# Two clamps to GpSimd, four weight splits to VectorE, and a later decode of the first weight blocks

## The chip, the cores and the metric

One core of a Trainium2 chip runs the whole program: one launch, inputs and output in the chip's memory. The metric is the device time of the program in microseconds. The median of three runs before the change is 835.16 us (833.45 to 838.1).

## What is computed

Three stages. The first is a linear attention with a decay per key channel, over 4 batches, 8 heads, 768 steps and 48 channels:

```python
for t in range(S):
    cur = np.einsum('bhd,bhe->bhde', u[None] * kt, vt)
    y[:, :, t] = np.einsum('bhd,bhde->bhe', rt, state + cur)
    state = wt[:, :, :, None] * state + np.einsum('bhd,bhe->bhde', kt, vt)
```

Its output, 3072 tokens by 384, goes through `h = x @ w_in`, `g = h * clip(h + 3, 0, 6) / 6`, `g @ w_out` with 2048 hidden columns, and then through a second feed-forward layer with 1024 hidden columns, a softmax-weighted `h`, a normalisation over the row with a gain, and a last product. The inputs of the attention are single precision. The weights are double precision in memory.

## The kernel before

**Attention.** The 768 steps are cut into 6 chunks of 128; a chunk of one batch is a tile, so there are 24 tiles, numbered chunk by chunk (tile `i` is batch `i % 4`). Each goes through six stages: `stw` (L410) clamps the decay to 0.75 to 1.25 and checks it on ScalarE; `st0` (L427) transposes decay and `r` on TensorE and forms running products with scans on VectorE; `st1` (L454) does the same for `k`, and forms `z = r * k * u` on GpSimd; `st2` (L495) makes the scores on TensorE and masks them into `am`; `st3` (L549) multiplies by `v`; `st4` (L603) writes the tile into the first feed-forward layer's input as a high and a low part. In the first four tiles one half of the masked scores is copied by ScalarE and then cut by GpSimd's affine select (L528). The clamped decay `wc` has one buffer, so a tile's clamp waits until the tile before has been transposed.

**Weights.** Each double is read as two 32-bit words. A block is 128 hidden columns of `w_in` and the matching rows of `w_out`, 768 values per partition, loaded by two transfers (`load_dec`, L25). `dec_a` (L35) clamps the high word, masks its sign (both on VectorE), and scales the clamped word on ScalarE. `dec_b` (L47) merges it with the sign and with the low word's top bits, two VectorE instructions (L50 and L53) that each read two tiles. `split` (L59) writes the high part on ScalarE and, as the difference, the low part on the engine that it is given (L61): GpSimd for every block. `w1_a` and `w1_b` (L354, L357) do this for the 16 blocks of the first layer; `w2_a` and `w2_b` for the 16 half-size blocks of the second, 384 values each. Raw words and decoded words have two buffers each.

**First feed-forward layer.** Six groups of 512 tokens times 16 blocks make 96 slots. In a slot `n`, `ffn_in` (L629) does nine products into `h`, ScalarE and VectorE make `t`, `gh` and `gl` of it (L643 to L647; `gl` on GpSimd in every other of the first 16 slots), and `ffn_out` (L650) does nine products two slots later. One attention tile goes through its stages for every four slots, so tile 4 and later ones run between the products. Slot `n` also decodes: `w1_b(n + LD)`, `w1_a(n + LD + 1)` and the load of block `n + LD + 2`, with `LD` 5 (L787 to L792). The second layer's weights are decoded in slots 78 to 94.

**Order.** The first four tiles and the first decodes run ahead of the slots in ten ticks (L753): in each tick every tile of the first four does its next stage (the tiles start at ticks 0, 2, 3 and 4), then the blocks of that tick's row of `decodes` follow, each with the rest of the block before it and the next load. In this part the queues of SP (which issues the loads) and of GpSimd keep the written order among themselves; on the other engines, and after `order.close()` on all, a scheduler chooses the order of the instructions from modelled costs. Each engine carries out its queue in order.

```python
decodes = {4: [0, 1], 5: [2], 6: [3], 7: [4], 8: [5]}
...
for m in decodes.get(tick, []):
    if m:
        w1_b(m - 1)
        w1_load(m + 1)
    w1_a(m)
```

The inputs of a tile have two buffers (tile 2's lie elsewhere), `v` from tile 4 on has four. `load_to` (L732) loads a later tile after `st1` in the ticks, and after `st2` in the slots.

Of the kernel before, what the change touches and what calls it, by code (L numbers as in the profile page):

```python
# [8 lines left out]
F32 = mybir.dt.float32  # L9
# [4 lines left out]
ALU = mybir.AluOpType  # L14
# [4 lines left out]
P = 128  # L19
W_LO, W_HI = 0.75, 1.25  # L20
SIGN = -(2**31)
HW_MAX = struct.unpack("<f", struct.pack("<I", 0x47EFF000))[0]
# [13 lines left out]
def dec_a(nc, pool, raw):  # L36

    f = pool.tile([P, raw.shape[1]], I32, tag="dec", name="dec", bufs=2)
    hw = raw[:, :, 1]
    nc.vector.tensor_scalar(  # L40
        out=f.bitcast(F32), in0=hw.bitcast(F32), scalar1=-HW_MAX, scalar2=HW_MAX, op0=ALU.max, op1=ALU.min
    )
    nc.vector.tensor_scalar(out=hw, in0=hw, scalar1=SIGN, scalar2=None, op0=ALU.bitwise_and)  # L43
    nc.scalar.activation(out=f.bitcast(F32), in_=f.bitcast(F32), func=ACTF.Copy, scale=2.0**-112)
    return f


def dec_b(nc, raw, f):

    nc.vector.scalar_tensor_tensor(  # L50
        out=f, in0=f, scalar=3, in1=raw[:, :, 1], op0=ALU.logical_shift_left, op1=ALU.bitwise_or
    )
    nc.vector.scalar_tensor_tensor(  # L53
        out=f, in0=raw[:, :, 0], scalar=29, in1=f, op0=ALU.logical_shift_right, op1=ALU.bitwise_or
    )
    return f.bitcast(F32)


def split(nc, src, hi, lo, eng):  # L59
    nc.scalar.activation(out=hi, in_=src, func=ACTF.Copy)  # L60
    eng.tensor_tensor(out=lo, in0=src, in1=hi.bitcast(F32), op=ALU.subtract)  # L61
# [206 lines left out]
def fast_path(  # L268
# [14 lines left out]
    nc = tc.nc  # L283
    B, H, S, D = r.shape
# [45 lines left out]
        out=causal.bitcast(F32), in_=ones, pattern=[[1, P]], compare_op=ALU.is_gt, fill=0.0, base=0,  # L330
# [3 lines left out]
    inp = right.enter_context(tc.tile_pool(name="inp", bufs=2, side="right"))  # L334
# [7 lines left out]
    w1_t = {}  # L342
    wst = {}
# [12 lines left out]

    def w1_b(m):  # L357
        w1_t[m] = w1p.tile([P, 2, WN], F32R, tag=f"w1_{m}", name="w1")
        split(nc, dec_b(nc, *wst.pop(m)), w1_t[m][:, 0, :], w1_t[m][:, 1, :], nc.gpsimd)


    s_st = []
# [30 lines left out]
    def load_v(i):  # L393
        g, b = divmod(i, B)
        if i < B:
            t = early(i, 1, H, D)
        else:
            t = inp.tile([P, H, D], F32, tag="v", name="v", bufs=4)
        nc.sync.dma_start(out=t, in_=v[b, :, g * C:(g + 1) * C, :].rearrange("h t d -> t h d"))
        at[i]["v"] = t  # L400

# [8 lines left out]
    def stw(i):  # L410
        a = at[i]
        wc = atp.tile([P, H, 64], F32, tag="wc", name="wc", bufs=1)
        flat = slice(0, H * 64 - 16)
        nc.vector.tensor_scalar(
            out=wc.rearrange("p h d -> p (h d)")[:, flat], in0=a["w"].rearrange("p h d -> p (h d)")[:, flat],
            scalar1=W_LO, scalar2=W_HI, op0=ALU.max, op1=ALU.min,
        )
        a["wc"] = wc
        junk = atp.tile([P, H, D], BF16, tag="junk", name="junk", bufs=1)
        nc.scalar.activation(  # L420
            out=junk, in_=a["w"][:, :, 0:D], func=ACTF.Relu, scale=-1.0, bias=b_lo, accum_out=chk[:, 3 * i:3 * i + 1]
        )
        nc.scalar.activation(
            out=junk, in_=a["w"][:, :, 0:D], func=ACTF.Relu, bias=b_hi, accum_out=chk[:, 3 * i + 1:3 * i + 2]
        )
# [309 lines left out]
            load_v(nxt[0])  # L735
            nxt[0] += 1

    LD = 5
    order = ctx.enter_context(ExitStack())
    order.enter_context(tc.manual_schedule(engines={mybir.EngineType.SP, mybir.EngineType.Pool}))  # L740
    load_in(0)
# [7 lines left out]
    w1_load(1)  # L749
    nxt[0] = 3  # L750
    starts = [0, 2, 3, 4]
    decodes = {4: [0, 1], 5: [2], 6: [3], 7: [4], 8: [5]}
    for tick in range(starts[-1] + 6):  # L753
        for i in range(B):
            s = tick - starts[i]
# [164 lines left out]
```

## Time and profile before

| | |
|---|---|
| median of three runs | 835.16 us |
| the profiled execution, its own time | 835.26 us |
| its span, from the first instruction to the last | 833.2 us |
| TensorE busy (share of the span) | 789.2 us (95%) |
| VectorE busy | 533.0 us (64%) |
| ScalarE busy | 350.0 us (42%) |
| GpSimd busy | 288.2 us (35%) |
| mean granted clock of TensorE | 0.958 of full speed |

In the profile PE is TensorE's products and PEld its weight loads, DVE is VectorE, ACT ScalarE, POOL GpSimd, SP the engine that issues loads and stores. Busy time is the time that an engine's instructions cover; an instruction that is held up inside its execution counts as busy. A line such as L50 is a line of the kernel, and `out<-in` are the program's names of tiles. In a row by line, the figures after the bar are the busy time of the group in us, the mean of one instruction in ns, and the idle time of the engine just before them with what ended it.

### The profile page before, as it was taken

The page shows a single profiled execution, that of the slowest core. Times are in us where ns is not written, and L with a number is a line of the kernel's source. Part 1 is how long each engine was busy: PE and PEld are TensorE (multiplying, and loading weights), DVE is VectorE, ACT ScalarE, POOL GpSimd, SP SyncE. Part 2 cuts the span into 40 slices and gives each one's busy share as a digit, 9 for nine tenths or more (in the row PEclk, how much of TensorE's full clock was granted, in tenths as well). Part 3 has the DMA queues.
Part 4 walks back from the last instruction along what each step waited for, and adds up shares of the span by engine and source line. Part 5 has one row for each costly group of instructions (what it writes and reads, how often), then busy time and mean ns, then how long its engine had stood idle before and what let it go on. Part 6 is the DMA issues. An engine that isn't in the chain of part 4 may idle for free.

```text
span 833.2 us, 12281 instructions
## 1 busy us (share of the span) xinstructions
PE 789.2 (95%) x4558; PEld 670.5 (80%) x4558; DVE 533.0 (64%) x988; ACT 350.0 (42%) x659; POOL 288.2 (35%) x379
## 2 busy tenths in 40 slices
PE   5779789999999999999999999998999999999996
PEld 5667577788888888888888888786789999999996
DVE  4989999756565555655556665699465555555552
ACT  2335644444334443343334333554443443344342
POOL 4385776634333332332233321122132222222210
PEclk7559997999999999999999999999999999999999
DMA  9765554214222322232222200433011111111101
GB/s 181 132 161 128 165 141 137 47 41 131 58 57 58 95 58 57 55 85 52 52 52 72 48 18 20 142 111 98 13 63 39 41 47 48 39 42 45 38 20 34
DMA packets 146117, 60.86 MB, mean 73 GB/s; under 512 B 103680, under 2 KB 140672, under 8 KB 146048
## 3 DMA queue, kind: packets, MB, share of 16 engines
q1 hardware_dynamic: 143456, 55.27, 27.1%
q10 hardware_dynamic: 2592, 4.72, 1.6%
q8 instruction: 38, 0.62, 0.3%
q14 instruction: 31, 0.25, 0.1%
HBM read 46.60 MB, written 13.37 MB: 72 GB/s over the span
## 4 chain that ended last, share of the span: by engine, by line
PE 73%; DVE 13%; issue 5%; ACT 3%; POOL 2%; DMA 2%; SPq 1%; POOLq 0%; ACTq 0%; DVEq 0%
PE y L659 19%; PE h L639 17%; PE po L856 12%; PE h L829 12%; DVE dec L50 3%; PE pt L843 2%; PE pa L519 2%; PE yt L570 2%; PE yt L576 2%; DVE dec L53 2%; PE kv L480 2%; DVE t L644 1%; DVE dec L40 1%; DVE raw L43 1%; DMA raw<-in_moe_w_in_dram 1%
## 5 line engine op out<-in xcount | busy, mean ns | idle before, releaser
L659 PE MATMUL y<-gh,w 128*128 128x512 f32 x576 | 204.4, 409 | 0.0
L639 PE MATMUL h<-xh,w 128*128 128x512 f32 x576 | 196.0, 394 | 4.6 <-DVE t L644 4.6
L639 PEld LDWEIGHTS h<-xh,w 128*128 128x128 f32 x576 | 109.0, 189 | 30.1 <-DVE t L644 7.1
L659 PEld LDWEIGHTS y<-gh,w 128*128 128x128 f32 x576 | 109.3, 190 | 27.8 <-issue 3.7
L643 ACT ACTIVATE t<-h,three 128x512 f32<-128x512 f32 x96 | 65.7, 685 | 151.2 <-PE h L639 151.2
L659 PE MATMUL y<-gl,w 128*128 128x512 f32 x288 | 114.3, 397 | 0.0
L639 PE MATMUL h<-xl,w 128*128 128x512 f32 x288 | 112.8, 392 | 0.0
L644 DVE SCALAR_TENSOR_TENSOR t<-t,h 128x512 f32<-128x512 f32 x96 | 65.3, 681 | 45.3 <-ACT t L643 45.3
L645 ACT ACTIVATE gh<-t 128x512 fp32r<-128x512 f32 x96 | 60.4, 629 | 73.9 <-DVE t L644 73.7
L647 DVE TENSOR_TENSOR gl<-t,gh 128x512 fp32r<-128x512 f32 x88 | 71.0, 807 | 29.6 <-ACT gh L645 28.0
L537 POOL TENSOR_TENSOR am<-ident,d 128x512 f32<-128x512 f32 x40 | 46.7, 1186 | 108.3 <-PE yt L576 107.4
L441 DVE TENSOR_TENSOR_SCAN q<-wt,ones 112x128 f32<-112x128 f32 x80 | 29.5, 409 | 69.3 <-PE wt L408 69.2
L67 DVE TENSOR_REDUCE nm<-h 128x1 f32<-128x1024 f32 x24 | 29.4, 1225 | 62.6 <-PE h L829 62.5
L856 PE MATMUL po<-w_oh,qh 128*128 128x384 f32 x192 | 67.0, 349 | 0.3 <-ACT qh L845 0.3
L856 PE MATMUL po<-w_oh,ql 128*128 128x384 f32 x192 | 65.2, 339 | 0.1
L856 PE MATMUL po<-w_ol,qh 128*128 128x384 f32 x192 | 65.0, 339 | 0.0
L639 PEld LDWEIGHTS h<-xl,w 128*128 128x128 f32 x288 | 54.5, 189 | 11.3
L659 PEld LDWEIGHTS y<-gl,w 128*128 128x128 f32 x288 | 55.0, 191 | 9.5 <-DVE gl L647 0.3
L845 ACT ACTIVATE qh<-pt 128x512 fp32r<-128x512 f32 x48 | 26.1, 595 | 79.0 <-PE pt L843 79.0
L829 PE MATMUL h<-w_ih,yl 128*128 128x512 f32 x144 | 56.6, 393 | 0.0
L829 PE MATMUL h<-w_il,yh 128*128 128x512 f32 x144 | 56.4, 392 | 0.0
L86 POOL TENSOR_TENSOR st<-st,mhalf 128x1 f32<-128x1 f32 x24 | 13.2, 552 | 124.0 <-DVE st L83 124.0
(123 smaller groups left out, 1483.8 us busy)
## 6 DMA issues: line engine op xcount, KB each, us to landing
raw<-in_moe_w_in_dram SPq DMA_DIRECT2D x24, 384.0 KB, 3.4
raw<-in_moe_w_out_dram SPq DMA_DIRECT2D x24, 384.0 KB, 4.1
w<-in_w_dram SPq DMA_DIRECT2D x24, 192.0 KB, 3.0
r<-in_r_dram SPq DMA_DIRECT2D x24, 192.0 KB, 3.2
k<-in_k_dram SPq DMA_DIRECT2D x24, 192.0 KB, 3.1
y1d<-ye ACTq DMA_DIRECT2D x18, 256.0 KB, 2.3
y<-y1d SPq DMA_DIRECT2D x24, 192.0 KB, 2.8
out_dram<-os SPq DMA_DIRECT2D x24, 192.0 KB, 1.9
```

The costliest lines, as they stand in the source:

```text
L67: nc.vector.tensor_reduce(out=nm, in_=h, axis=AX.X, op=ALU.max, negate=True)
L441: nc.vector.tensor_tensor_scan(out=q[0:DP, hp, 0:C][:, ::-1], data0=wt[0:DP, hp, :][:, ::-1], data1=ones[0:DP, :], initial=1.0, op0=ALU.mu ...
L537: nc.gpsimd.tensor_tensor(out=am, in0=ident.unsqueeze(1).to_broadcast([P, HP, C]), in1=dv[:, hh, :].unsqueeze(2).to_broadcast([P, HP, C]), ...
L639: nc.tensor.matmul(out=h, lhsT=a, rhs=b, start=(j == 0), stop=(j == len(ops) - 1))
L643: nc.scalar.activation(out=t, in_=h, func=ACTF.Relu, bias=three)
L644: nc.vector.scalar_tensor_tensor(out=t, in0=t, scalar=6.0, in1=h, op0=ALU.min, op1=ALU.mult)
L645: nc.scalar.activation(out=gh, in_=t, func=ACTF.Copy)
L647: eng.tensor_tensor(out=gl, in0=t, in1=gh.bitcast(F32), op=ALU.subtract)
L659: nc.tensor.matmul(out=y_ps[g][c], lhsT=a, rhs=b, start=(m == 0 and j == 0), stop=(m == M1 - 1 and j == 2))
L829: nc.tensor.matmul(out=h[:, fs], lhsT=a[:, c, :], rhs=b_[:, c, fs], start=(j == 0), stop=(j == len(ops) - 1))
L845: nc.scalar.activation(out=qh[:, ms, :], in_=pt, func=ACTF.Copy)
L856: nc.tensor.matmul(out=po, lhsT=x[:, m, :], rhs=y[:, m, :], start=(n == 0), stop=(n == 3 * M2 - 1))
```

## The change

Five edits. The clamp of the high words (`dec_a`, used by both layers' blocks) is issued by GpSimd, with its two bounds in the other order. The low part of the first four blocks (`m < B`, and `B` is 4) is formed on VectorE. The decay clamp is on GpSimd from tile 2 on. `v` has three buffers. Blocks are decoded four slots ahead, not five, and the ticks 4, 5, 7, 8 and 9 hold one block each, so that the loads of blocks 2 to 5 come in ticks 5, 7, 8 and 9.

```diff
--- before.py
+++ after.py
@@ -37,8 +37,8 @@
 
     f = pool.tile([P, raw.shape[1]], I32, tag="dec", name="dec", bufs=2)
     hw = raw[:, :, 1]
-    nc.vector.tensor_scalar(
-        out=f.bitcast(F32), in0=hw.bitcast(F32), scalar1=-HW_MAX, scalar2=HW_MAX, op0=ALU.max, op1=ALU.min
+    nc.gpsimd.tensor_scalar(
+        out=f.bitcast(F32), in0=hw.bitcast(F32), scalar1=HW_MAX, scalar2=-HW_MAX, op0=ALU.min, op1=ALU.max
     )
     nc.vector.tensor_scalar(out=hw, in0=hw, scalar1=SIGN, scalar2=None, op0=ALU.bitwise_and)
     nc.scalar.activation(out=f.bitcast(F32), in_=f.bitcast(F32), func=ACTF.Copy, scale=2.0**-112)
@@ -356,7 +356,7 @@
 
     def w1_b(m):
         w1_t[m] = w1p.tile([P, 2, WN], F32R, tag=f"w1_{m}", name="w1")
-        split(nc, dec_b(nc, *wst.pop(m)), w1_t[m][:, 0, :], w1_t[m][:, 1, :], nc.gpsimd)
+        split(nc, dec_b(nc, *wst.pop(m)), w1_t[m][:, 0, :], w1_t[m][:, 1, :], nc.vector if m < B else nc.gpsimd)
 
 
     s_st = []
@@ -395,7 +395,7 @@
         if i < B:
             t = early(i, 1, H, D)
         else:
-            t = inp.tile([P, H, D], F32, tag="v", name="v", bufs=4)
+            t = inp.tile([P, H, D], F32, tag="v", name="v", bufs=3)
         nc.sync.dma_start(out=t, in_=v[b, :, g * C:(g + 1) * C, :].rearrange("h t d -> t h d"))
         at[i]["v"] = t
 
@@ -411,9 +411,10 @@
         a = at[i]
         wc = atp.tile([P, H, 64], F32, tag="wc", name="wc", bufs=1)
         flat = slice(0, H * 64 - 16)
-        nc.vector.tensor_scalar(
+        eng = nc.vector if i < 2 else nc.gpsimd
+        eng.tensor_scalar(
             out=wc.rearrange("p h d -> p (h d)")[:, flat], in0=a["w"].rearrange("p h d -> p (h d)")[:, flat],
-            scalar1=W_LO, scalar2=W_HI, op0=ALU.max, op1=ALU.min,
+            scalar1=W_HI, scalar2=W_LO, op0=ALU.min, op1=ALU.max,
         )
         a["wc"] = wc
         junk = atp.tile([P, H, D], BF16, tag="junk", name="junk", bufs=1)
@@ -735,7 +736,7 @@
             load_v(nxt[0])
             nxt[0] += 1
 
-    LD = 5
+    LD = 4
     order = ctx.enter_context(ExitStack())
     order.enter_context(tc.manual_schedule(engines={mybir.EngineType.SP, mybir.EngineType.Pool}))
     load_in(0)
@@ -749,7 +750,7 @@
     w1_load(1)
     nxt[0] = 3
     starts = [0, 2, 3, 4]
-    decodes = {4: [0, 1], 5: [2], 6: [3], 7: [4], 8: [5]}
+    decodes = {4: [0], 5: [1], 7: [2], 8: [3], 9: [4]}
     for tick in range(starts[-1] + 6):
         for i in range(B):
             s = tick - starts[i]
```

## Rows read from the trace of the kernel before

**Rows 1.** The page's 40 slices: TensorE's busy tenths and its granted clock in tenths.
```profile
PE   5779789999999999999999999998999999999996
...
PEclk7559997999999999999999999999999999999999
```

**Rows 2.** Busy us by stretch: length, PE, PEld, DVE, ACT, POOL; granted clock, DMA share, GB/s.
```profile
4.00:63.40 59.40, 43.60 (x197) 38.82 (x197) 45.68 (x84) 20.74 (x46) 30.58 (x41) 0.56 0.81 161
63.40:160.00 96.60, 83.92 (x512) 67.89 (x511) 92.57 (x132) 51.18 (x98) 67.31 (x59) 0.92 0.48 128
160.00:528.00 368.00, 367.17 (x2347) 304.54 (x2346) 214.27 (x400) 145.99 (x279) 117.94 (x155) 1.00 0.25 60
528.00:590.00 62.00, 58.41 (x251) 46.11 (x250) 55.63 (x99) 33.06 (x63) 17.43 (x16) 1.00 0.35 108
```

**Rows 3.** TensorE's waits, 4 to 63 us: us in total, times, longest.
```profile
PE wt L408 <- DVE wc L414: 6.4, 3, 4.7
PE yt L563 <- POOL am L528: 6.3, 3, 2.8
```

**Rows 4.** GpSimd in order of time, 28 to 58 us: start, length, instruction.
```profile
31.10 1.82 POOL L61 TENSOR_TENSOR w<-dec,w 128x768 fp32r<-128x768 f32 x1 [13.59 <-ACT w L60]
32.87 0.95 POOL L528 TENSOR_SCALAR_AFFINE_SELECT am<-am 128x512 f32<-128x512 f32 x1
...
52.93 1.81 POOL L61 TENSOR_TENSOR w<-dec,w 128x768 fp32r<-128x768 f32 x1 [1.72 <-ACT w L60]
54.69 1.36 POOL L528 TENSOR_SCALAR_AFFINE_SELECT am<-am 128x512 f32<-128x512 f32 x1
```

**Rows 5.** TensorE's waits, 63 to 160 us.
```profile
PE ktp L469 <- DVE q L460: 9.1, 3, 4.9
```

**Rows 6.** VectorE in order of time, 20 to 56 us.
```profile
20.11 0.53 DVE L40 TENSOR_SCALAR dec<-raw 128x768 f32<-128x768 f32 x1
...
27.74 0.93 DVE L50 SCALAR_TENSOR_TENSOR dec<-dec,raw 128x768 int32<-128x768 int32 x1
...
31.45 1.88 DVE L43 TENSOR_SCALAR raw<-raw 128x768 int32<-128x768 int32 x1
...
53.62 1.94 DVE L50 SCALAR_TENSOR_TENSOR dec<-dec,raw 128x768 int32<-128x768 int32 x1
```

**Rows 7.** GpSimd lines L725 and L528: ns min/median/max of each instruction.
```profile
L725 POOL TENSOR_SCALAR yh<-y x24: 512/514/523, 195.8 to 792.7; 128x384 fp32r<-128x384 f32 x24
...
L528 POOL TENSOR_SCALAR_AFFINE_SELECT am<-am x4: 636/956/1360, 14.0 to 54.7; 128x512 f32<-128x512 f32 x4
```

**Rows 8.** VectorE by line, 63.4 to 160 us: busy us, mean ns, idle before.
```profile
L50 DVE SCALAR_TENSOR_TENSOR dec<-dec,raw 128x768 int32<-128x768 int32 x12 | 17.3, 1438 | 1.5 <-ACT dec L44 1.5
L53 DVE SCALAR_TENSOR_TENSOR dec<-raw,dec 128x768 int32<-128x768 int32 x12 | 15.4, 1283 | 0.1
L43 DVE TENSOR_SCALAR raw<-raw 128x768 int32<-128x768 int32 x12 | 9.6, 800 | 0.1
L40 DVE TENSOR_SCALAR dec<-raw 128x768 f32<-128x768 f32 x11 | 9.0, 820 | 0.0
L644 DVE SCALAR_TENSOR_TENSOR t<-t,h 128x512 f32<-128x512 f32 x13 | 8.8, 675 | 0.2 <-ACT t L643 0.2
L647 DVE TENSOR_TENSOR gl<-t,gh 128x512 fp32r<-128x512 f32 x6 | 7.8, 1298 | 1.0 <-ACT gh L645 1.0
...
L414 DVE TENSOR_SCALAR wc<-w 128x496 f32<-128x496 f32 x4 | 4.7, 1165 | 0.0
```

**Rows 9.** VectorE's clamps, 528 to 590 us; TensorE's waits, 528 to 600.
```profile
L40 DVE TENSOR_SCALAR dec<-raw 128x384 f32<-128x384 f32 x16 | 7.2, 449 | 0.8 <-DMA gcol<-in_moe_g_ln_dram 0.6 <-DMA raw<-in_moe_w_in_dram 0.2
...
PE h L639 <- DVE t L644: 3.6, 5, 1.5
```

**Rows 10.** GpSimd's split by line, 63.4 to 160 us.
```profile
L61 POOL TENSOR_TENSOR w<-dec,w 128x768 fp32r<-128x768 f32 x12 | 23.3, 1938 | 15.7 <-ACT w L60 15.7
```

**Rows 11.** ScalarE's high part by line, 63.4 to 160 us.
```profile
L60 ACT ACTIVATE w<-dec 128x768 fp32r<-128x768 f32 x12 | 10.1, 844 | 13.9 <-DVE dec L53 13.9
```

## Prediction, made before the changed kernel was run

> **What bounds the kernel now.** I read the page's slices first, then the busy time by stretch, then TensorE's waits in the stretches where it is not full, and last the engine that it waits for. The slices [rows 1] show TensorE at nine tenths or more almost everywhere after the first eighth, and its clock at the lower level (1.2 GHz) in most of the first eight slices. The stretches [rows 2] put figures on that. From 160 to 528 us TensorE is busy 367.17 of 368 us: nothing on another engine is worth anything there. What can be won lies in three places: 4 to 63.4 us (the first four attention tiles), where TensorE is busy 43.6 of 59.4 us at a granted clock of 0.56; 63.4 to 160 (the first thirteen slots of the feed-forward part), where it idles 12.7 us and the clock is 0.92; and 528 to 590 (decode of the second weights), where it idles 3.6.
>
> In the first place two waits of TensorE can be touched: 6.4 us for the clamped decay, of which 4.7 is the very first tile, which the change leaves alone, and 6.3 us for the masked scores `am` [rows 3]. The scores are late because of an order: GpSimd's affine select (L528) stands behind the split of a weight block (L61), and begins within 0.1 us of that split's end, three times in this part; the first and the last pair stand in [rows 4]. The split itself waits for VectorE's decode, through ScalarE.
>
> In the second place VectorE is the bound: busy 92.57 of 96.6 us [rows 2], and TensorE waits for its scans and products (9.1 us for the scaled keys) [rows 5]. But much of VectorE's busy time is not work. The sign mask took 1.88 us at 31.45 and the first merge 1.94 at 53.62, each over a GpSimd split and each ending soon after it; undisturbed, the merge took 0.93 and the clamp, of the mask's shape, 0.53 [rows 4, 6]. GpSimd waits likewise: the select at 54.69 took 1.36, over the end of that merge [rows 4], against 0.64 undisturbed [rows 7]. So GpSimd's instructions and those of VectorE that read two tiles, or one tile at double rate, take turns. Instructions with an operand in PSUM do not: `t` holds 675 ns on average over thirteen [rows 8].
>
> **The change, part by part.** The sum is made against the profiled execution, 835.26 us (span 833.2, 2.1 outside it); the median of the runs is 0.1 lower, so the two are one number here.
>
> *Price of a clamp on GpSimd.* Not in the trace. A two-operation pass over 128x384 takes 514 ns, the select over 128x512 0.64 us [rows 7]: 0.12 us per 128 columns, so 768 columns come to 0.9 us as an estimate. Bounds: 0.51 (half the columns) and 1.81, the split, which reads two tiles of this width [rows 4]. I take 0.9, since a clamp reads one tile; a decay clamp (496 columns) comes to 0.62.
>
> *First part, 4 to 63.4 us.* Removed from GpSimd: four splits. Nothing of VectorE's decode then stands ahead of the select, so TensorE's three waits for it, 6.3 us [rows 3], can go. Removed from VectorE: the decay clamps of tiles 2 and 3, which TensorE waited for (6.4 less 4.7 leaves 1.7), and the clamps of the blocks. Added to VectorE: splits over 768 columns, two tiles read, so a merge's 0.93 each, three ahead of the feed-forward part: 2.8 us, and that is what is late next, since VectorE is busy 45.7 of the 59.4 us and the scans stand in its queue too. Added to GpSimd: two decay clamps, each waiting there for its tile's transfer, with tile 1's or tile 2's `z` queued behind, whose row sum VectorE wants only for that tile's output; and the block clamps, one ahead of each of the second and third tiles' selects. They wait for a transfer alone, block 0's issued before tile 2's. Sum: 6.3 + 1.7 - 2.8 = 5.2, say **-5**. Bounds: 0 if the clamps hold the selects as the splits did, -8 if the added VectorE work falls into its own idle time (59.4 - 45.7 = 13.7 us [rows 2]).
>
> *Second part, 63.4 to 160.* Off VectorE: eleven block clamps at 9.0 us and four decay clamps at 4.7, together 13.7, turns included [rows 8]. On GpSimd: 11 x 0.9 + 4 x 0.62 = 12.4 us, to a busy time of 67.3 [rows 2]. The remaining turn-takers (both merges, mask, `gl`) now lose 12 x 0.51 + 12 x 0.35 + 12 x 0.27 + 6 x 0.63 = 17.3 us to GpSimd, by their means against 0.93, 0.93, 0.53 and 0.67 (`gl` as `t`) [rows 6, 8]. If loss goes with GpSimd's busy time, it grows by 12.4/67.3, 3.2 us; if each new GpSimd microsecond is one of VectorE's, by 12.4. Neither end is near, so I take the middle, 7.8: -13.7 + 7.8 = -5.9. Against that, only blocks 0 to 2 are surely decoded when this stretch begins, not 0 to 3: two merges and a split, 2.8 us. **-3**; bounds -10.5 and +1.5. A gain passes to TensorE one for one while it has idle time left (12.7 us; and a granted 0.92 means that some 96.6 x 0.08 / 0.5 = 15 us ran at the lower level [rows 2]).
>
> By the Trainium skill (GPSIMD Engine Reference, § 1 and § 8) GpSimd shares its SBUF interfaces with VectorE and contends with VectorE instructions that run in a two-port mode or read two SBUF inputs. By that rule taken strictly the loss is the 12.4 end and this part ends at +1.5; by the rows' middle it is -3. The rows agree on which instructions contend; how long the one-input clamp holds the other engine no row shows.
>
> *Third part, 528 to 590.* Sixteen clamps of 449 ns leave VectorE, 7.2 us; TensorE's waits for `t` in it total 3.6 [rows 9]. GpSimd is busy 17.4 of 62 us and takes sixteen of 0.51 [rows 2, 7]. Half of the 3.6, as in the second part: **-1.5**; bounds +1 and -3.6.
>
> *At nothing.* The decay clamps after 160 us: TensorE is full, and GpSimd is busy 118 of 368 us [rows 2]; were that cover gone, tiles would be late. The swapped order of the two bounds in a clamp: the same instruction. Three buffers of `v`: tile i+2 takes the buffer of tile i-1, last read three slots earlier; were it not free, the transfers behind it on SP would wait too. Blocks four slots ahead, not five: four slots are 4 x 7.4 = 30 us (thirteen `t` in 96.6 us [rows 2, 8]) against a decode of some 6 us. On SP the two transfers of block 2 go behind tile 4's four, and block 3's behind tile 5's, which wait for tile 3's buffers; block 3 is first needed in the fourth slot, 22 us into the second part, and that hides it.
>
> Sum: 835.3 - 5 - 3 - 1.5 = 825.8.
>
> **Rivals.** *Turns are strict.* Second part +1.5, third 0, first -5: 831.8. For it: the waits that last to the other engine's end [rows 4, 6]. It is the rule of the Trainium skill named in the second part, taken to its end. Against it: in the second part VectorE has `t`, scans and products to run meanwhile, and GpSimd stood idle 29 of 96.6 us. *The select still waits* (the clamps, in GpSimd's written order, stand where the splits stood, and wait for a transfer): first part 0, 830.8. Against it: the clamp needs a transfer, not a chain over three engines. *Relief is full:* -8, -8 and -2.5, 816.8; for it, that the clamps were disturbed most, 1.17 us on average for a decay clamp [rows 8], which is the smaller of the two. *Slower: the decode becomes a chain through GpSimd.* If the clamp of the next block stands behind the split of this one in GpSimd's queue, then merge, merge, high part, split, clamp and scaling follow one another: 1.44 + 1.28 + 0.84 + 1.94 + 0.9 + 0.84 = 7.2 us [rows 8, 10, 11], the scaling taken as the high part, a pass over the same columns, and what else GpSimd does in a slot, (67.3 - 23.3)/13 = 3.4, stands between; with half of it 8.9 a block against 7.4 a slot now. Twelve blocks: +18, less 5 from the first part, 848. It decides once more than some 0.6 us of other GpSimd work falls into the chain (12 x 0.4 takes back the first part's 5). For it: GpSimd already sat 15.7 us before splits, waiting for the high part [rows 10]. Against it: the clamp needs only a transfer that came long before, so it can go ahead of the split. *The change does not do what it says* is excluded: the engines are named in the code.
>
> **Numbers.** Half a per cent, 4.2 us, is about what a measurement can tell, so faster means under 831.0. The forecast has 0.41, full relief 0.16, strict turns 0.17, the select still waiting 0.13, the chain 0.13. Faster: the first two, and near half of the select's case, which stands on the line: 0.63. Slower: the chain, 0.13. The rest, 0.24, is the same. The range goes from full relief with a little below it, 815, to strict turns with no gain in the third part and some loss of the first, 837; the chain and the tails stay out.
>
> **What would show it.** Right: in the first part no split on GpSimd, TensorE's wait for `am` under 2 us, the first L639 before 60 us; between there and full TensorE, VectorE's merges at means of 1.4 and 1.3 us or a little more, its share below 95%, GpSimd's up by some 12 us. Strict turns: merges well over 1.6 us and VectorE as full as before. Chain: VectorE idle with the merge waiting for the scaling, the scaling for the GpSimd clamp. The forecast is wrong if L639 starts no earlier, or if TensorE's idle time from there to full load grows.

## The result, and the profile after

The changed kernel takes 843.52 us (median of four runs, 842.82 to 845.75) beside 834.54 for the kernel before on the same chip: a ratio of 1.0105 with an interval of 1.0069 to 1.0141. It is about 1% slower; the prediction was 825.8, and 843.5 lies above its range, which ended at 837. The profiled execution took 842.82 us, against 835.26 before: 7.6 us more.

The busy time by stretch, with columns as in [rows 2]. The first stretch ends at the first product of the feed-forward part, the second at the start of the fourteenth `t` (161.69 us before, 168.91 after); the third and fourth answer to the last two of [rows 2].

```profile
4.00:56.00 52.00, 42.80 (x197) 39.38 (x197) 36.33 (x73) 18.54 (x45) 25.31 (x44) 1.00 0.82 152
56.00:168.90 112.90, 87.39 (x525) 71.27 (x525) 91.83 (x125) 55.49 (x100) 82.57 (x76) 0.91 0.45 123
168.90:535.00 366.10, 365.27 (x2334) 302.98 (x2335) 195.41 (x383) 143.49 (x277) 121.20 (x170) 1.00 0.27 61
535.00:597.00 62.00, 58.42 (x249) 45.62 (x248) 49.26 (x82) 33.55 (x62) 26.76 (x32) 1.00 0.35 108
```

The granted clock of the first row is not to be compared: no clock record lies ahead of 57.8 us in this trace, and where there is none, full speed is printed.

The same work of the kernel before, from its first feed-forward product (63.38 us) to its fourteenth `t`, for the second row:

```profile
63.40:161.70 98.30, 85.62 (x525) 69.33 (x525) 93.61 (x134) 52.29 (x99) 68.50 (x60) 0.92 0.48 126
```

The first stretch became 7.4 us shorter, and the second, with the same 525 products, 14.6 longer. The difference of 7.2 at the fourteenth `t` is what stands at the end: from there to the last `t` it moves by 0.4. So nearly the whole loss is made between 56 and 169 us. VectorE did 1.8 us less in the second stretch and stood idle 21.1 of 112.9 us, where it had been idle 4.7 of 98.3. It is no longer the bound that it was; GpSimd's busy time rose by 14.1.

What the engines wait for in that stretch, 56 to 165 us (us in total, times, longest), first ScalarE's:

```profile
ACT dec L44 <- POOL dec L40: 22.4, 7, 5.2
ACT w L60 <- DVE dec L53: 17.0, 10, 3.8
```

then VectorE's:

```profile
DVE raw L43 <- POOL dec L40: 10.4, 6, 4.3
DVE d L514 <- POOL z L464: 3.2, 1, 3.2
```

and TensorE's, where [rows 5] had 9.1 us for the scaled keys first:

```profile
PE kv L481 <- ACT ktok L474: 10.5, 3, 6.4
PE ktp L470 <- DVE q L461: 7.6, 2, 6.4
```

The same waits of the kernel before, from 63 to 160 us:

```profile
ACT dec L44 <- DVE dec L40: 4.4, 3, 3.3
PE kv L480 <- ACT ktok L473: 1.1, 2, 0.8
```

One wait has grown and one is new: ScalarE's scaling (L44) waits 22.4 us for the clamp on GpSimd (before, for VectorE's clamp, 4.4), and VectorE's sign mask (L43), which overwrites in place the words that the clamp reads, waits 10.4. And `ktok`, a copy by ScalarE, holds TensorE up for 10.5 us; before it was 1.1.

One place shows how they hang together. GpSimd in order of time from 82 us, gapless for 13 us:

```profile
82.45 2.12 POOL L61 TENSOR_TENSOR w<-dec,w 128x768 fp32r<-128x768 f32 x1
84.53 1.76 POOL L538 TENSOR_TENSOR am<-ident,d 128x512 f32<-128x512 f32 x1
86.26 2.01 POOL L648 TENSOR_TENSOR gl<-t,gh 128x512 fp32r<-128x512 f32 x1
...
91.36 1.80 POOL L61 TENSOR_TENSOR w<-dec,w 128x768 fp32r<-128x768 f32 x1
93.13 0.86 POOL L40 TENSOR_SCALAR dec<-raw 128x768 f32<-128x768 f32 x1
```

ScalarE at the same time, with the idle time before an instruction and what ended it:

```profile
94.03 0.84 ACT L44 ACTIVATE dec<-dec 128x768 f32<-128x768 f32 x1 [4.82 <-POOL dec L40]
94.78 0.53 ACT L474 ACTIVATE ktok<-ktp 128x448 f32<-128x448 f32 x1
```

and TensorE:

```profile
95.36 1.81 PE L481 MATMUL kv<-early,ktok 128*112 128x96 f32 x8 [6.37 <-ACT ktok L474]
```

The clamp runs at 93.13. It could have begun at 85.4: the buffer that it writes was free when the split at 82.45 ended, and its transfer, which is issued when the second merge of the block before last has freed the buffer of raw words, landed at 85.44. The merge and the later of its two loads:

```profile
79.21 1.63 DVE L53 SCALAR_TENSOR_TENSOR dec<-raw,dec 128x768 int32<-128x768 int32 x1
81.30 0.48 SPq L31 DMA_DIRECT2D raw<-in_moe_w_out_dram  x1
```

The other 7.7 us are GpSimd's queue: `am`, `gl`, `z`, a decay clamp and the next split stand ahead of the clamp. ScalarE stands at the scaling from 89.2, and `ktok`, whose input TensorE had finished at 86.9, is queued behind it. TensorE stands still for 6.37 us, and its granted clock is at the lower level (1.2 GHz) from 91.9 to 98.8 us.

### The profile page after: what moved, and what is told of

Read it like the earlier page. It is cut to its first block, busy times and chain, and to the rows that moved or that the text cites. A ratio compares the mean times of both kernels' runs of the same rounds, so it can differ in the third digit from the quotient of the medians.

```text
span 840.7 us, 12325 instructions
## 1 busy us (share of the span) xinstructions
PE 790.6 (94%) x4558; PEld 673.0 (80%) x4558; DVE 498.0 (59%) x938; ACT 350.6 (42%) x659; POOL 310.6 (37%) x429
## 3 DMA queue, kind: packets, MB, share of 16 engines
q1 hardware_dynamic: 143456, 55.27, 27.1%
## 4 chain that ended last, share of the span: by engine, by line
PE 73%; POOL 8%; DVE 7%; issue 4%; DMA 4%; SPq 2%; ACT 1%; POOLq 0%; DVEq 0%; ACTq 0%
PE y L660 19%; PE h L640 17%; PE po L857 12%; PE h L830 12%; PE pt L844 2%; PE pa L520 2%; PE yt L571 2%; DVE dec L50 2%; POOL dec L40 2%; PE yt L577 2%; PE kv L481 1%; DVE dec L53 1%; SPq L389 1%; POOL w L61 1%; DMA raw<-in_moe_w_in_dram 1%
## 5 line engine op out<-in xcount | busy, mean ns | idle before, releaser
L640 PE MATMUL h<-xh,w 128*128 128x512 f32 x576 | 197.6, 397 | 7.4 <-DVE t L645 7.2
L640 PEld LDWEIGHTS h<-xh,w 128*128 128x128 f32 x576 | 109.6, 190 | 34.2 <-DVE t L645 11.1
L640 PE MATMUL h<-xl,w 128*128 128x512 f32 x288 | 113.4, 394 | 0.0
L648 DVE TENSOR_TENSOR gl<-t,gh 128x512 fp32r<-128x512 f32 x88 | 65.3, 742 | 24.7 <-ACT gh L646 23.2
L640 PEld LDWEIGHTS h<-xl,w 128*128 128x128 f32 x288 | 54.9, 191 | 11.0
L830 PE MATMUL h<-w_ih,yl 128*128 128x512 f32 x144 | 56.6, 393 | 0.0
```

The source lines that it names most:

```text
L640: nc.tensor.matmul(out=h, lhsT=a, rhs=b, start=(j == 0), stop=(j == len(ops) - 1))
L648: eng.tensor_tensor(out=gl, in0=t, in1=gh.bitcast(F32), op=ALU.subtract)
L830: nc.tensor.matmul(out=h[:, fs], lhsT=a[:, c, :], rhs=b_[:, c, fs], start=(j == 0), stop=(j == len(ops) - 1))
```

## The experiments

Each kernel was timed in three rounds beside the kernel before, and a ratio is to that kernel on the same chip, with its 95% interval. Letters of theories are those of the texts; in the first eight, Q is GpSimd's queue with the clamp in it, L the lead of four slots, T the turns, D the stream of decodes, H the head start.

**One part undone.** The block clamps back on VectorE, all else as changed:

```diff
-    nc.gpsimd.tensor_scalar(
+    nc.vector.tensor_scalar(
         out=f.bitcast(F32), in0=hw.bitcast(F32), ...
...
```

> The changed kernel with the clamp of every weight block back on VectorE; the other four edits stay. Theory Q (the GpSimd clamp is the cost: GpSimd's queue is long between 56 and 165 us, the clamp comes late, and it stands at the head of VectorE's and ScalarE's queues, so that the key copy and the scans behind it are late): 826 to 832 us, the start of L640 within 2 us of the changed kernel's 56.0, ScalarE's wait for the clamp gone (22.4 us in the changed kernel), TensorE's waits for the key copy under 4 us (10.5 in the changed kernel). Theory L (blocks are decoded four slots ahead, not five, so the decode is late): 840 to 845 us. Theory T (one-input GpSimd instructions take VectorE's turns): about 832 to 836, since the clamp costs VectorE what it saves.

Measured: 1.0005 (0.9981 to 1.0029), so the clamp's place is worth the 1%. By the ratio that is 834.9 beside 834.5: not the 826 to 832 that Q had named, but within T's 832 to 836. Without the clamp the other parts together bring nothing. Of the waits between 56 and 165 us, the mask's is gone, and the two others are back near what they were:

```profile
ACT dec L44 <- DVE dec L40: 7.0, 7, 2.6
PE kv L481 <- ACT ktok L474: 1.6, 2, 0.8
```

This kernel is called the first run below.

The clamp on GpSimd for blocks 0 to 4 (those of the ticks) alone:

```diff
...
-        wst[m].append(dec_a(nc, dec, wst[m][0]))
+        wst[m].append(dec_a(nc, dec, wst[m][0], nc.gpsimd if m <= B else None))
```

> The changed kernel with the GpSimd clamp for blocks 0 to 4 of the first layer alone (those of the ticks); all later blocks of both layers are clamped on VectorE. Theory Q: 826 to 832 us, within 2 us of the kernel with every clamp on VectorE, since GpSimd's queue is short in the first part. Theory L: 840 to 845 us. Theory T: as the kernel with every clamp on VectorE, 832 to 836.

Measured: 1.0013 (0.9996 to 1.0031), as with no clamp there. What costs are the eleven clamps of the slots: the second layer's are undone here too, but from the fourteenth `t` on the changed kernel had lost 0.4 us only.

**One part alone.** The clamp for all blocks, on the kernel before:

```diff
-    nc.vector.tensor_scalar(
+    nc.gpsimd.tensor_scalar(
...
```

> The kernel before with the clamp of every weight block on GpSimd and nothing else changed. Theory Q: slower, 843 to 855 us, because the second part loses some 15 us as in the changed kernel and the first part has no gain to set against it. Theory L: 830 to 837 us, since the lead of five slots is kept. Theory T: 835 to 841.

Measured: 1.0128 (1.0094 to 1.0163), as Q had it and neither L nor T; the table, the splits and the decay clamps are not needed for the loss. ScalarE's wait between 56 and 165 us:

```profile
ACT dec L44 <- POOL dec L40: 27.1, 11, 5.6
```

The changed kernel with the lead of five slots:

```diff
-    LD = 4
+    LD = 5
-    decodes = {4: [0], 5: [1], 7: [2], 8: [3], 9: [4]}
+    decodes = {4: [0], 5: [1], 7: [2], 8: [3], 9: [4, 5]}
```

> The changed kernel with blocks five slots ahead again (LD 5, and block 5 started in tick 9). Theory Q: 838 to 848 us, little changed, since the lead is not what is short. Theory L: 826 to 832 us. Theory T: 840 to 844.

Measured: 1.0128 (1.0097 to 1.016). A block more in hand does not help; L falls.

The other three parts, each on the kernel before. The lead and the ticks:

```diff
-    LD = 5
+    LD = 4
-    decodes = {4: [0, 1], 5: [2], 6: [3], 7: [4], 8: [5]}
+    decodes = {4: [0], 5: [1], 7: [2], 8: [3], 9: [4]}
```

> The kernel before with the later decode alone (LD 4 and the new ticks). Theory D (the sixteen blocks' decode is a stream through VectorE that ends the second part: TensorE runs full some 7 to 12 us after the last merge, so a block that is decoded later costs its delay, and an earlier first L640 gives nothing by itself): the first L640 at 57 to 61 us instead of 63.4, the last merge of the first layer's blocks 3 to 8 us later than 150.5, total 837 to 843. Theory H (the head start counts): total 828 to 833.

Measured: 0.9982 (0.9962 to 1.0002), so no gain that is clear. By the ratio it is 833.0 beside 834.5, at H's upper end, and not D's 837 to 843, though the first product and the last merge came when D had said, at 57.6 and 156.4 us. The splits of blocks 0 to 3:

```diff
-  ... w1_t[m][:, 1, :], nc.gpsimd)
+  ... w1_t[m][:, 1, :], nc.vector if m < B else nc.gpsimd)
```

> The kernel before with the low parts of the first four blocks on VectorE and nothing else changed. Theory D: the decode of the early blocks is not put off, the masked scores no longer stand behind a split, and VectorE has 4 x 0.9 us more: first L640 at 58 to 62 us, the last merge within 3 us of 150.5, total 830 to 836. Theory H: 828 to 833, the head start in full.

Measured: 1.0041 (1.0021 to 1.0061), slower, against both theories. The decay clamps:

```diff
-        nc.vector.tensor_scalar(
+        eng = nc.vector if i < 2 else nc.gpsimd
+        eng.tensor_scalar(
...
```

> The kernel before with the decay clamps from tile 2 on on GpSimd and nothing else changed. Theory D: VectorE is rid of some 5 us of disturbed clamps by 160 us, and the last merge comes up to 4 us earlier: 830 to 835. Theory Q (a long queue on GpSimd makes its results late): 835 to 840, since the decay clamp waits there for transfers with other work behind it.

Measured: 0.9979 (0.9958 to 1.0), as D had it and not Q. Splits and decay clamps together, the last two diffs in one:

> The kernel before with both, the four splits on VectorE and the decay clamps on GpSimd, block clamps on VectorE and the old ticks: the changed kernel without its clamp and its table. Theory D: 826 to 833, faster than before, since nothing puts the decode off. Theory Q: 833 to 838. Should it come out slower than before, neither the clamp nor the table is the whole of the loss.

Measured: 0.9941 (0.9915 to 0.9967), again as D had it, and faster than either alone. The parts do not add up: 1.0041 and 0.9979 would give 1.002. With the table on top (the first run) it is 1.0005, though the table alone gave 0.9982. Each edit also changes the order that the scheduler chooses for the rest, which may be why; no run shows it.

**The clamp's place in the queue.** In each slot the next block's clamp is issued ahead of the rest of the block before it:

```diff
+        if n + LD + 1 < M1:
+            w1_a(n + LD + 1)
         if n + LD < M1:
             w1_b(n + LD)
-        if n + LD + 1 < M1:
-            w1_a(n + LD + 1)
```

on the changed kernel:

> The changed kernel, but in every slot the next block's clamp is issued ahead of the rest (merges, split) of the block before it, so that in GpSimd's queue the clamp stands one split earlier. Theory Q (the loss is the place of the clamp in GpSimd's queue, at whose result the in-order queues of ScalarE and VectorE stand still): 834 to 839 where the changed kernel is 843.5 and the kernel before 834.5, and ScalarE's wait for the clamp between 56 and 165 us falls from 22.4 to under 11 us. Rival T (the loss is the clamp's time on GpSimd, which VectorE loses by turns, wherever the clamp stands): 842 to 846, though the wait of ScalarE may fall. Rival S (any other order of issue moves the time by half a per cent either way): 839 to 848, and the run with the same edit but the clamp on VectorE moves as much.

then splits, decay clamps and block clamps on the kernel before, without and with that swap, and the control with the clamp on VectorE:

> Three of the four parts on the kernel before: splits of blocks 0 to 3 on VectorE, decay clamps on GpSimd, block clamps on GpSimd; LD 5 and the old ticks. The same without the block clamp stood at 0.9941 of the kernel before. If the block clamp costs what it cost in the two other pairs (1.0 and 1.3%), this one is at 1.004 to 1.008, 838 to 841 beside a kernel before of 834.5. If the later table is what makes the GpSimd clamp dear (the changed kernel has one block less in hand), it is at 0.997 or less, 832 and below.

> The run just named (splits, decay clamps and block clamps moved, old table) with the next block's clamp issued ahead of the rest of the block before it. Theory Q: it gives back at least half of what the block clamp costs there, so 0.994 to 1.000, 829 to 834.5 beside a kernel before of 834.5. Rival T: no gain over the run just named, 838 to 841.

> The control: splits and decay clamps moved, block clamps left on VectorE, old table, with the next block's clamp issued ahead of the rest of the block before it. Theory Q: nothing to win, since no clamp stands behind a split; within 0.3% of the same kernel without the swap, so 0.991 to 0.997, 827 to 832. Rival S: it moves by as much as the two runs with the swap and the clamp on GpSimd do.

Measured: 1.0062 (1.0034 to 1.0089); 1.0014 (0.9991 to 1.0038) and 1.0008 (0.9988 to 1.0028); 0.9962 (0.994 to 0.9985). The second, without the swap, lies between the two cases that its text had named. The swap took 0.4% back on one base, within the overlap of the intervals, and nothing on the other; the control moved by 0.2% the other way, so that S, a mere change of order, stands too. ScalarE's wait in the first of the four did not fall:

```profile
ACT dec L44 <- POOL dec L40: 23.5, 10, 6.4
```

so this way of issuing did not take the chain away, and the four runs do not tell Q from T. The clamps of the eleven slots did begin nearer to the moment when both their transfer had landed and their buffer was free, 26.5 us late in total where it was 34.0 in the changed kernel. But that moment hangs on the merge and the split of the block before last, since there are two buffers of each kind, and an earlier place in the queue does not move it.

**The waiting instructions issued later.** The mask at the head of the merges, on the changed kernel; then mask and scaling; then the mask on the old table, with the clamp on GpSimd and on VectorE:

```diff
 def dec_a(nc, pool, raw):
...
-    nc.vector.tensor_scalar(out=hw, in0=hw, scalar1=SIGN, scalar2=None, op0=ALU.bitwise_and)
 def dec_b(nc, raw, f):
+    hw = raw[:, :, 1]
+    nc.vector.tensor_scalar(out=hw, in0=hw, scalar1=SIGN, scalar2=None, op0=ALU.bitwise_and)
```

> The changed kernel with the sign mask (it overwrites in place the words that the clamp reads, so it must wait for the clamp) issued a step later, at the head of the merges instead of right behind the clamp. Theory W (what the GpSimd clamp costs is that VectorE, in order, stands still at the mask: 10.4 us of waits between 56 and 165 us, all of them new): the wait falls under 3 us and the time to 833 to 838, where the changed kernel is 843.5 and the kernel before 834.5. Theory V (it is ScalarE's standing at the scaling, 22.4 us, that holds TensorE up): the wait of VectorE falls, the time stays at 840 to 844.

> The changed kernel with the mask and ScalarE's scaling both issued a step later, at the head of the merges, so that neither queue meets the clamp's result early. Theory V: 831 to 837, with ScalarE's wait for the clamp under 5 us. Theory W: like the run with the mask alone, 833 to 838. Rival C (the decode is a chain, and a scaling that starts later makes each block later): slower than the run with the mask alone, 840 or more, VectorE waiting for the scaling at the first merge.

> Splits, decay clamps and block clamps moved, old table (1.0014 of the kernel before as it stood), with the mask issued at the head of the merges. Theory W: it gives back most of the 0.7% by which it is behind the same kernel with the clamp on VectorE (0.9941), so 0.993 to 0.998, 829 to 833 beside 834.5. Theory V: 0.999 to 1.003.

> The control: splits and decay clamps moved, block clamps on VectorE, old table, mask issued at the head of the merges. There no mask waits for a clamp on another engine. Theories W and V: within 0.3% of 0.9941, which is 827.5 to 832 beside 834.5. If it moves by as much as the run with the GpSimd clamp does, the gain is that of the order of issue and not of the wait.

Measured: 1.0089 (1.0059 to 1.0118), 1.0068 (1.0038 to 1.0098), 1.0072 (1.0048 to 1.0096) and 0.9926 (0.9906 to 0.9946). By the ratios that is 841.9, 840.2, 840.5 and 828.3 beside 834.5. W misses its times in the three runs with the clamp on GpSimd. V has its time in the first, and misses it in the second and third. But the condition of neither was met: in the first of these runs the mask (now L50) and the scaling (L43) still waited for the clamp,

```profile
DVE raw L50 <- POOL dec L40: 7.5, 4, 3.0
```

and, on ScalarE's side,

```profile
ACT dec L43 <- POOL dec L40: 17.8, 8, 3.9
```

so the clamp comes late even for an instruction that asks a step later. Rival C of the second run, that a later scaling makes each block later, is not borne out: it is not slower than the run with the mask alone, and its first merge waited 1.2 us for the scaling, after 1.5. In the profiled executions of the first and the second of these runs, and of the swap on the changed kernel, TensorE idled 24.6, 22.7 and 22.8 us in the second stretch, against 25.5, but was busy 90.9, 94.0 and 90.3 us for the same 525 products, against 87.4, at granted clocks of 0.88, 0.84 and 0.85, against 0.91: what was won in waits went, in these executions, to the clock. The control, with splits and decay clamps moved and the block clamps left on VectorE, has the lowest ratio of the study.

**Load and chain apart.** With the clamps on VectorE, GpSimd gets for each clamp of the first layer a pass over the same block's low words, in two halves of 384 columns, into a scratch tile (`gho`) that nothing reads; then the changed kernel with those passes on VectorE:

```diff
...
         wst[m].append(dec_a(nc, dec, wst[m][0]))
+        for _ in range(2):
+            nc.gpsimd.tensor_scalar(
+                out=gho, in0=wst[m][0][:, 384 * _:384 * _ + 384, 0], scalar1=1.0, scalar2=-1.0, op0=ALU.min, op1=ALU.max
+            )
```

> The changed kernel with its block clamps back on VectorE (1.0005 of the kernel before), plus on GpSimd, at the place of each of the sixteen clamps of the first layer, a pass over the block's low words (two instructions of 384 columns into a scratch tile that nothing reads). GpSimd then has the clamps' time, but nobody waits for it. Theory C (the cost is the chain: merge, high part, split and the next clamp wait for one another across three in-order queues): within 0.4% of the same kernel without the passes, 0.998 to 1.004, 833 to 838 beside a kernel before of 834.5. Rival T (the cost is the time on GpSimd itself, by turns with VectorE and by all that then comes later from GpSimd): 1.007 or more, 840 and up, and VectorE's merges at means over 1.6 us.

> The changed kernel as it stands (block clamps on GpSimd), plus on VectorE, at the place of each of the sixteen clamps, the same pass over the low words: VectorE has its old load again, and only the chain through GpSimd is left of the change of engine. Theory C (VectorE stands idle for the chain anyway, so its relief brought nothing): 1.008 to 1.014, 841 to 846. Rival R (the relief of VectorE is worth something and only part of what it brought was lost): slower than the changed kernel by near the added time, 16 passes of some 0.6 us, so 1.016 or more, 848 and up.

Measured: 1.0098 (1.0067 to 1.0129) and 1.021 (1.0168 to 1.0251). So T and R have their times, and C, as the only cause, falls: time on GpSimd whose result nobody reads costs 0.9% (from 1.0005), and VectorE's relief is worth something, since 1.05% is lost when an equal number of passes is put back. T's other sign did not come: the merges' means were 1.46 and 1.18 us, not over 1.6. The passes were not quite free of waits either. With the passes on GpSimd, the loads into the words' buffers waited 1.1 us for them, and a clamp on VectorE 3.2 for a split on GpSimd; with the passes on VectorE, one load waited 7.6 for a pass. And the passes were longer than the clamps. By line between 56 and 170 us (busy us, mean ns, idle before), the run with the passes on GpSimd:

```profile
L359 POOL TENSOR_SCALAR gho<-raw 128x384 f32<-128x384 int32 x25 | 23.3, 931 | 2.1 <-DMA raw<-in_moe_w_in_dram 1.6
```

the run with the passes on VectorE:

```profile
L359 DVE TENSOR_SCALAR gho<-raw 128x384 f32<-128x384 int32 x26 | 20.1, 775 | 0.1
```

beside the clamps of the changed kernel,

```profile
L40 POOL TENSOR_SCALAR dec<-raw 128x768 f32<-128x768 f32 x13 | 14.2, 1099 | 5.8 <-DVE e L448 4.6 <-DMA raw<-in_moe_w_out_dram 1.2
```

and those of the first run, on VectorE:

```profile
L40 DVE TENSOR_SCALAR dec<-raw 128x768 f32<-128x768 f32 x13 | 11.0, 847 | 0.0
```

In proportion, as an estimate, and with 1% taken as 8.4 us: the clamps' 14.2 us on GpSimd cost 7.8 x 14.2/23.3 = 4.8, and the 11.0 us off VectorE bring 8.8 x 11.0/20.1 = 4.8. Load and relief cancel. From 1.0005 to 1.0105 are 8.4 us, so some 8 us are left for the third term: that other queues now wait for the clamp. The intervals of the four ratios make that 8 give or take 3, and the sum takes the three terms as independent, which the parts of the change above were not. The windows from the first feed-forward product to the fourteenth `t` show the two kinds of loss. The first run:

```profile
56.60:165.30 108.70, 88.77 (x525) 70.97 (x525) 99.26 (x138) 56.45 (x102) 71.89 (x64) 0.89 0.49 126
```

the run with the passes on GpSimd:

```profile
56.50:170.80 114.30, 91.60 (x527) 72.63 (x527) 103.45 (x139) 56.94 (x102) 94.19 (x89) 0.88 0.46 120
```

the run with the passes on VectorE and the clamps on GpSimd:

```profile
57.90:177.70 119.80, 92.11 (x525) 73.75 (x525) 105.37 (x150) 55.05 (x98) 91.64 (x77) 0.86 0.43 114
```

Against the first run's 108.70 us with 9.4 of idle VectorE, the passes on GpSimd add 5.6 us, of which 4.2 is VectorE's busy time: nearly the same instructions took longer, which is what turns would do. The changed kernel adds 4.2 us to it with 7.4 less of busy time on VectorE and 11.6 more of idle. With the chain and the old load, VectorE is busy 6.1 longer and idle 5.0 longer. (The profiled executions are single ones, and executions of one kernel differ by several tenths of a per cent; sizes are taken from the ratios, the kind of loss from the windows.)

**All pairs.** Five pairs differ in the clamp's engine alone:

| else as in | clamp on VectorE | on GpSimd | difference |
|---|---|---|---|
| the kernel before | 1 | 1.0128 | +1.3% |
| splits, decay | 0.9941 | 1.0014 | +0.7% |
| the same, next clamp first | 0.9962 | 1.0008 | +0.5% |
| the same, mask late | 0.9926 | 1.0072 | +1.5% |
| splits, decay, table, `v` | 1.0005 | 1.0105 | +1.0% |

All have one sign, 1.0% on average. What the five have in common shows in their traces between the first feed-forward product and the fourteenth `t`: with the clamp on GpSimd, VectorE is busy 0.9 to 7.4 us less but idle 6.4 to 17.3 us more, and from 56 to 169 us ScalarE waits 18.2 to 27.1 us for the clamp, against 4.4 to 11.3, while the mask's wait, of 10.0 to 12.2, is new. TensorE's wait for `ktok` is not common: it grows by 8.9 us in the last pair and by 0.7 to 2.8 in the others. The table (in all but the first with the three buffers of `v`) costs -0.2% alone, which is not clear of nothing, +0.6% on splits and decay clamps, and +0.9% with the block clamps too.

## Why the prediction was wrong

*First part, -5 (0 to -8): right in itself, but it did not last.* -7.4, as the first L640 starts at 55.99 us where L639 started at 63.38 [rows 2]; no split stands on GpSimd, and of the waits of [rows 3] the one for the masked scores is gone, while the first tile's stays:

```profile
PE wt L408 <- DVE wc L415: 4.7, 1, 4.7
PE pa L520 <- DVE e L452: 3.6, 1, 3.6
```

The block clamps stand ahead of the selects and cost what was priced, 0.9 and 0.62, in these rows of GpSimd in order of time, against the pairs of [rows 4] (in the second part the mean of a block clamp is 1.10, as shown above):

```profile
24.50 0.60 POOL L415 TENSOR_SCALAR wc<-w 128x496 f32<-128x496 f32 x1 [5.00 <-DMA w<-in_w_dram]
25.18 0.87 POOL L40 TENSOR_SCALAR dec<-raw 128x768 f32<-128x768 f32 x1
28.75 0.63 POOL L529 TENSOR_SCALAR_AFFINE_SELECT am<-am 128x512 f32<-128x512 f32 x1 [2.71 <-DMA w<-in_w_dram]
```

*Second part, -3 (-10.5 to +1.5): wrong, and this is the step that failed.* It came out at +14.6. VectorE's busy time was taken for the only limit of the stretch. Two things went into the +14.6. The first is the head start: the sum let the first part's gain pass to the end, and put only 2.8 us for the block less decoded. With the clamps on VectorE (the first run) the first product comes at 56.6, 6.8 us early, and yet the second stretch takes 10.4 more; with the later table alone, 5.8 early and 5.9 more, so that nothing is won or lost:

```profile
57.60:161.70 104.10, 87.30 (x527) 70.20 (x527) 98.31 (x139) 55.87 (x102) 77.06 (x62) 0.93 0.50 135
```

In that run VectorE is busy 98.31 of the stretch's 104.10 us, where it was busy 93.61 of 98.30: the decode that no longer stands ahead of the first product is done behind it. The second is the clamp. The terms for it were VectorE's work removed and turns added; the sum had no term for waiting on it, and the two it did have cancel at about 4.8 us each (an estimate, above), where -13.7 and +7.8 had been put down for block and decay clamps together. With the chain, idle time took the place of what fell away: VectorE stood idle 21.1 us of the stretch, where it had been idle 4.7. The merges' means, forecast at 1.4 and 1.3 or a little more, came out at 1.6 and 1.2, the first at the edge of the sign for strict turns; VectorE's share was below 95% as forecast, and GpSimd's busy time up by 14 instead of 12:

```profile
L50 DVE SCALAR_TENSOR_TENSOR dec<-dec,raw 128x768 int32<-128x768 int32 x13 | 21.1, 1623 | 0.9 <-ACT dec L44 0.3
L53 DVE SCALAR_TENSOR_TENSOR dec<-raw,dec 128x768 int32<-128x768 int32 x14 | 17.2, 1232 | 0.2
L43 DVE TENSOR_SCALAR raw<-raw 128x768 int32<-128x768 int32 x13 | 12.5, 964 | 10.5 <-POOL dec L40 10.4
```

So most signs that looked at one engine were met. The one named for a failure was too: TensorE's idle time in the stretch went from 12.7 to 25.5 us.

*The slower rival, 848 at 0.13: the right place, half the mechanism.* It said that the next clamp stands behind the split, and that the scaling then waits for it; both are in the rows at 91.36, 93.13 and 94.03. It was turned down with "the clamp needs only a transfer that came long before, so it can go ahead of the split": that it can does not mean that the queue's order has it so. Nor had the transfer come long before: in the place shown it landed 4.6 us after the merge that freed its buffer, and the clamp began 7.7 us after that. Over the eleven clamps of the slots, the clamp begins 0.2 to 7.7 us after transfer and buffer were ready, 34.0 in total. The rival saw the decode alone. The merge hardly waits for the scaling (0.3 us above); VectorE stands at the in-place mask instead, and what reaches TensorE in this kernel is other work queued behind the scaling, `ktok` above all. In the other pairs it is not `ktok`, and by which path the loss reaches TensorE there was not followed.

*Turns are strict, 831.8:* the shape was right in that GpSimd's time costs even when nobody reads its result. The Trainium skill (GPSIMD Engine Reference, § 1 and § 8) names this contention with VectorE's instructions; the run with the passes agrees, with VectorE's busy time up by 4.2 us for 23.3 us on GpSimd: `gl`, which reads two tiles, took 2.4 us more in six instructions, the clamps 1.7 and the first merges 1.6, while the mask took 1.4 less and `t`, with an operand in PSUM, kept its mean of 677 ns. Neither the 4.2 nor the 7.8 us of the ratio is one for one, so strict turns are not what these passes met. *The select still waits* and *full relief* did not come about.

*Third part, -1.5 (+1 to -3.6):* within the bounds, +0.4. VectorE's clamps of [rows 9] are gone, but the mask waits 7.6 us there,

```profile
L43 DVE TENSOR_SCALAR raw<-raw 128x384 int32<-128x384 int32 x16 | 6.8, 427 | 7.6 <-POOL dec L40 7.6
```

and TensorE's wait for `t` went from 3.6 to 3.4.

*At nothing.* The stretch to 535 us stayed full of products, 365.27 of 366.10 us. The lead of four slots as such costs nothing that shows (1.0128 with five). The ticks' table was put at +2.8 us in the second part; alone it is -0.2%, on top of the other parts +0.6 and +0.9%. Why it costs there and not alone is open: the last merge of the first layer ends at 158.7 us in the first run and at 148.6 with splits and decay clamps alone, but at 156.4 in the run of the table alone too, which lost nothing. The three buffers of `v` were not tried by themselves. One reading of [rows 1] was off, and no term hangs on it: the lower clock fills two of the first eight slices and parts of others, not most of them.

*What stays open.* That some 8 us hang on the wait and not on the load rests on the load scaling with its time, on terms that add up, and on single ratios with intervals of 0.2 to 0.4% either way. Which link costs most, the scaling at ScalarE's head or the mask at VectorE's, was not told apart, since no run took the waits away while leaving the clamp on GpSimd; a third buffer of raw and decoded words, which would give the clamp a block's lead, was not tried. Which of the scheduler's orders brings splits and decay clamps together to 0.9941, when they gave 1.0041 and 0.9979 alone, is not explained.

## What to carry to other kernels

Moving a step off the busiest engine has three terms, not two: what that engine gets back, what the other engine's added time takes from it, and what now waits for the result. For the third, take the step's new place in its engine's queue, then every in-order queue that meets its result (those that only overwrite its input included), and list what stands behind that instruction there: here, in one place, it was a copy of 0.53 us whose delay left TensorE idle for 6.37. Ask also when the step could run at the earliest: with two buffers, that hangs on the block before last. To tell load from waiting, leave the step where it was and give the other engine an equal pass that nobody reads, and look whether loads wait for that pass.

## What the runs showed of the hardware

A pass of GpSimd over 384 columns of every second word took between 0.52 and 1.43 us, with a median of 0.84; the one at 109.28 us, with VectorE idle, took 0.54, and the longest, at 69.86, spans the whole of a first merge of 0.93:

```profile
L359 POOL TENSOR_SCALAR gho<-raw x32: 516/842/1430, 24.8 to 158.7; 128x384 f32<-128x384 int32 x32
```

GpSimd is held up too: in the run with the passes on VectorE, its product `z` (here L470) took 2.6 us on average, against 1.4 in the changed kernel, where one beside an idle VectorE took 0.99 (at 44.27 us):

```profile
L470 POOL TENSOR_TENSOR z<-z,u_bc 128x384 f32<-128x384 f32 x5 | 13.1, 2623 | 0.3
```

Two of the five took 4.2 and 5.0 us, over merges, mask, `gl` and two of the passes one after another on VectorE; the splits kept their 1.9 us. So this is not the passes' doing alone.

The order of issue alone moved a kernel by as much as single parts of the change: with the same work on the same engines, 1.0014 became 1.0072 by the mask's place. A single part below half a per cent cannot be read from one such kernel.
